# Soft-capped attention before two feed-forward layers: conversions by GpSimd, six key buffers, one transfer for sums, and the last pair's row sums on TensorE

## The chip, the cores and the metric

One Trainium2 chip, and one of its cores. The time is what the device takes for one launch, in microseconds (us). The kernel before takes 515.05 us, the median of 3 runs (514.95 to 515.98).

## The reference

Twelve heads in each of two batches, 448 positions, 64 channels a head. With `q` and `k` scaled so that the scores spread widely:

```python
scores = (q @ k.T) / sqrt(64)
scores = cap * tanh(scores / cap)              # cap is an input, 30.0
attn = exp(scores - max(scores))               # the kernel leaves the maximum out where cap bounds it
attn = attn / (sum(attn) + 1e-9)
x = (attn @ v), heads side by side             # 896 tokens x 768
x = relu(x @ w_in) ** 2 @ w_out                # 768 -> 2048 -> 768
x = silu(x @ w2_in) @ w2_out                   # 768 -> 2048 -> 768
```

All is float32 outside; the weights come as 64-bit floats and are turned into pairs of 16-bit floats (a high and a low part) on the chip.

## The kernel before

**Attention.** The 24 heads are 12 pairs; a pair shares a tile of 128 partitions, one head in the upper 64 channels and one in the lower. Two pairs make a round (`m`, 0 to 5), and a round has seven blocks of keys: A0, A1, A2 for the first pair, B0, B1, B2 for the second (128 keys each), and C, which holds the last 64 keys of both pairs, the first pair's in partitions 0 to 63 and the second pair's in 64 to 127. The 42 blocks are taken two at a time: a step `h` of the loop issues the scores of two blocks (TensorE, `scores`, L570), their tanh and exp (ScalarE, L584 and L679), and the products with the values of the two blocks of the step before (`values`, L586).

**Row sums.** VectorE adds the exponentials of a pair's blocks into `total` (`add`, L603), and TensorE multiplies `total` by a block of equal numbers (`ones`), which gives the sum over keys, repeated over rows. For the rounds 0 to 4 one bank of PSUM holds four sums (`add_up`, L615). VectorE copies it to `sm`, four transfers turn its four rows of 448 into a tile `st` of 32 partitions by 56 (L641), VectorE inverts that (L646, L647), it goes to DRAM (`scratch`, L648) and comes back repeated over 64 partitions (`rb`, L654), and the pair's output is multiplied by it (L659). For the last two pairs (10 and 11) the sums go through `add_up_pair` (L625) to a full bank each, `sump`, and VectorE inverts 128x448 numbers at once (`last_sums`, L662).

**What sets the order.** Each engine works its instructions in the order in which the program issues them, and so does the queue of SyncE, from which all the large transfers start. A tile takes the place of an older tile of its kind (`bufs` says how many there are), and waits for that tile's last reader. Keys and queries of a pair are one tile `qk`, with four places; `pr.load` (L513) is issued in the steps in which block C or B2 of a round is scored, for the two pairs of the next round.

**Weights.** `Stream` loads a weight tile (`raw`, three places, 768 KB each), takes its upper half as a 16-bit float into `top` (the tile `zeros`, one place; `head`, L306), lets VectorE shift the lower bits and join them (`shift`, L313, which writes `u`), and splits `u` into the high and low parts `hl`. Twelve such steps are issued one by one in the steps 5 to 16 of the attention (`ws.step`, L718), the first four conversions among them. After the attention a planner takes over: it keeps a clock for ScalarE and VectorE and, beside each piece of TensorE's work, issues the step that is open and due first (`chunk`, L467). The parts of the input `x0` that are still to be made are steps with due times too (`x0.late`).

**Feed-forward.** The first four output tiles are four sums of products (`plain`, L991): six units of twelve products first, of which four use only the pairs 0 to 7 and two need the pairs 8 to 11, then the next two tiles from whole inputs. TensorE's four banks for them are emptied by ScalarE before they are taken again.

Of the kernel before, what the change touches and what calls it, by code (L numbers as in the profile page):

```python
# [8 lines left out]
F32 = mybir.dt.float32  # L9
# [17 lines left out]
def softcap_attention_relu2_silu(  # L27
# [12 lines left out]
    nc = tc.nc  # L40
# [201 lines left out]
    class Stream:  # L242
# [53 lines left out]
        def turn_steps(self, i):  # L296
# [5 lines left out]
            def raw():  # L302
                self.load_to(i)
                return self.raw[i]

            def head():  # L306
                nc.scalar.activation(  # L307
                    top.bitcast(F16).rearrange("p (n w) -> p n w", w=2)[:, :, 1],
                    raw().bitcast(BF16).rearrange("p (n w) -> p n w", w=4)[:, :, 2],
                    AF.Copy,  # L310
                )

# [8 lines left out]

            a = Step("A", 1.4 * WT, head, [self.turned[i - BENT]] if i >= BENT else [])
            b = Step("D", WT, shift, [a], self.room)
# [182 lines left out]
    class Pairs:  # L506
# [6 lines left out]
        def load(self, i):  # L513
            t = self.pool.tile([128, 2, S], F32, tag="qk", bufs=4, name=f"qk{i}{self.tag}")
            nc.sync.dma_start(t[:, 0], q[i])
            nc.sync.dma_start(t[:, 1], k[i])
            self.qk[i] = t
# [18 lines left out]
    def attention_bounded(att, spool, ws, x0):  # L536
# [66 lines left out]
        def add(m, x):  # L603
            e, i = ex[m, x], None if x == "C" else pair_of(m, x)
            if x in ("A1", "B1"):
                t = total[i] = att.tile([128, 2, S], F32, tag=f"total{x[0]}", bufs=2, name=f"total{i}")
                nc.vector.tensor_tensor(t, ex[m, x[0] + "0"], e, op=ALU.add)  # L607
            if x == "A2" or x == "B2" and m < NQ - 1:
                nc.vector.tensor_tensor(total[i], total[i], e, op=ALU.add)  # L609
            if x in ("C", "B1"):  # L610
                b = int(x == "B1")
                t = total[2 * m + b][head(b)]
                nc.vector.tensor_tensor(t, t, ex[m, "C"][head(b)], op=ALU.add)  # L613
# [10 lines left out]

        def add_up_pair(i, parts):  # L625
            s = sums["p", i] = bank(f"sump{i}")
            for n, t in enumerate(parts):
                for j in range(2):
                    nc.tensor.matmul(
                        s[head(j), :S], lhsT=one, rhs=t[:, j], start=(n == 0), stop=(n == len(parts) - 1)  # L630
                    )

# [3 lines left out]
        def evacuate_sums(m):  # L636
            t = att.tile([128, S], F32, tag="sm", bufs=2, name=f"sm{m}")
            nc.vector.tensor_copy(t, sums.pop(m)[:, :S])
            st[m] = att.tile([32, S // 8], F32, tag="st", bufs=2, name=f"st{m}")
            for r in range(4):  # L640
                nc.sync.dma_start(  # L641
                    st[m][8 * r : 8 * r + 8], t[32 * r : 32 * r + 1].rearrange("o (a f) -> o a f", a=8)
                )

# [29 lines left out]
        for h in range(len(groups) + 1):  # L674
            if h < len(groups):
# [4 lines left out]
                for m, x in groups[h]:  # L680
                    if x in ("A0", "B0"):
                        i = pair_of(m, x)
                        if i + 2 < NP2:
                            pr.load_v(i + 2)
                    if x in ("C", "B2") and m + 1 < NQ:
                        pr.load(2 * m + 2 + (x == "B2"))
            if h == 1:
# [11 lines left out]
            for m, x in groups[h - 1] if h else []:  # L699
                values(m, x)  # L700
            for m, x in older:
                if x == "B2":
# [4 lines left out]
                    for b in range(2):  # L707
                        todo.append((lambda i=2 * m + b: normalise(i), h + 4 + 2 * b))
                if x == "C" and m == NQ - 1:
                    add_up_pair(last, [total[last]])  # L710
            if h in loads:
# [5 lines left out]
            if 5 <= h < 17:  # L717
                ws.step()  # L718
        add_up_pair(last + 1, [total[last + 1], ex[NQ - 1, "B2"]])
        for f, _ in todo:  # L720
            f()
        nc.scalar.activation(cell(last + 1), px.pop(last + 1)[:, :S], AF.Copy)
        x0.late(last_sums(last), last_sums(last + 1))

# [680 lines left out]
```

## Time and profile before

| what | value |
|---|---|
| median of 3 runs | 515.05 us |
| the profiled execution, its own time | 514.26 us |
| its span | 512.5 us |
| mean granted clock of TensorE | 0.992 of full speed |
| TensorE, matmuls | 501.1 us busy (98%), 2741 |
| VectorE | 353.0 us busy (69%), 668 |
| ScalarE | 337.2 us busy (66%), 516 |
| GpSimd | 24.1 us busy (5%), 28 |
| attention | from 5.4 us to about 90.6 us |
| feed-forward part | from about 90.6 us to the end |

The shares are means over stages with different limits, and a matmul counts as busy to its modelled end, so that 98% doesn't say that no time is lost. What is lost stands in the rows as a gap between the starts of TensorE's instructions, or in brackets behind an instruction: the time that its engine sat idle before it, and what ended that.

### The profile page before, as it was taken

To read this page: it belongs to the slowest core of one execution; us is meant where nothing else is said; L and a number is where in the kernel's file an instruction comes from. 1 tells how busy PE (TensorE), PEld (TensorE's weight loads), DVE (VectorE), ACT (ScalarE), POOL (GpSimd) and SP (SyncE) were. 2 spreads that over 40 slices of the span, in tenths; PEclk is the share of its full clock that TensorE was granted. 3 is DMA by queue.
4 is the path that set the end of the run, shared out by engine and by line. 5 is a ranking of instruction groups with operands and counts; after the bars stand their busy time and mean duration, and the time that the engine had idled before them with its cause. 6 is when DMAs were issued, how large, how long until landed. Compare 5 with 4: busy or idle time off the path is not lost.

```text
span 512.5 us, 7246 instructions
## 1 busy us (share of the span) xinstructions
PE 501.1 (98%) x2741; PEld 251.6 (49%) x2741; DVE 353.0 (69%) x668; ACT 337.2 (66%) x516; POOL 24.1 (5%) x28
## 2 busy tenths in 40 slices
PE   8999998999999999999999999999999999999995
PEld 4332232445555555555555555555666555556562
DVE  0769996898878677776779887889376278673110
ACT  5999898397778874448886757787555467860000
POOL 1003334300000000000000000000000000000000
PEclk9999999999999999999999999999999999999998
DMA  8546651233352355442453211336466013502111
GB/s 269 203 140 174 213 165 34 68 123 124 125 176 77 111 173 201 126 134 83 153 185 112 76 63 62 124 123 201 169 189 225 19 66 121 181 5 78 49 47 51
DMA packets 19357, 64.26 MB, mean 125 GB/s; under 512 B 2674, under 2 KB 11122, under 8 KB 19314
## 3 DMA queue, kind: packets, MB, share of 16 engines
q1 hardware_dynamic: 19280, 63.72, 37.8%
q8 instruction: 23, 0.38, 0.3%
q14 instruction: 20, 0.16, 0.1%
q0 software_dynamic: 32, 0.00, 0.0%
q10 hardware_dynamic: 2, 0.00, 0.0%
HBM read 60.88 MB, written 2.79 MB: 124 GB/s over the span
## 4 chain that ended last, share of the span: by engine, by line
PE 83%; DVE 10%; DMA 3%; SPq 2%; issue 1%; ACT 0%; DVEq 0%
PE yb_4f L858 4%; PE yb_5f L858 4%; PE yb_3f L858 4%; PE yb_0f L858 4%; PE yb_1f L858 4%; PE yb_2f L858 4%; PE yd_1f L1155 3%; PE yd_6f L1155 3%; PE yd_5f L1155 3%; PE yd_4f L1155 3%; PE yd_3f L1155 3%; PE yd_2f L1155 3%; PE yd_0f L1155 3%; SPq L641 2%; PE ha_1f L858 2%; DMA st<-sm 2%
## 5 line engine op out<-in xcount | busy, mean ns | idle before, releaser
L584 ACT ACTIVATE e_A<-s_A 128x896 f32<-128x896 f32 x18 | 16.0, 930 | 5.4 <-PE s_A L576 5.4
L584 ACT ACTIVATE e_B<-s_B 128x896 f32<-128x896 f32 x18 | 16.1, 936 | 1.4 <-PE s_B L576 1.2
L679 ACT ACTIVATE e_B<-e_B 128x896 f32<-128x896 f32 x18 | 16.7, 974 | 0.0
L679 ACT ACTIVATE e_A<-e_A 128x896 f32<-128x896 f32 x18 | 16.7, 970 | 0.0
L613 DVE TENSOR_TENSOR total<-total,e_C 64x896 f32<-64x896 f32 x12 | 13.4, 1114 | 0.4
L189 DVE SCALAR_TENSOR_TENSOR x1f<-yaf,x1f 128x448 f16<-128x448 f32 x15 | 9.2, 623 | 3.5 <-ACT x1f L799 3.4
L218 ACT ACTIVATE junk<-x0f 128x896 bf16<-128x896 f16 x6 | 5.7, 944 | 7.1 <-DVE x0f L804 6.8
L609 DVE TENSOR_TENSOR total<-total,e_A 128x896 f32<-128x896 f32 x6 | 8.2, 1360 | 0.3
L810 DVE TENSOR_TENSOR yaf<-yaf 128x448 f32<-128x448 f32 x12 | 7.2, 620 | 0.6 <-ACT yaf L799 0.6
L607 DVE TENSOR_TENSOR total<-e_A,e_A 128x896 f32<-128x896 f32 x6 | 6.6, 1103 | 1.2 <-ACT e_A L679 1.2
L799 ACT ACTIVATE x1f<-yaf 128x448 f16<-128x448 f32 x12 | 6.8, 570 | 0.8 <-DVE yaf L810 0.6
L646 DVE TENSOR_SCALAR st<-st,gcap 32x56 f32<-32x56 f32 x5 | 2.4, 471 | 7.0 <-DMA st<-sm 7.0
L1169 DVE SCALAR_TENSOR_TENSOR ycf<-yd_0f,ycf 128x384 f32<-128x384 f32 x2 | 1.1, 558 | 8.4 <-PE yd_0f L1155 8.4
L607 DVE TENSOR_TENSOR total<-e_B,e_B 128x896 f32<-128x896 f32 x6 | 6.7, 1122 | 0.0
L858 PEld LDWEIGHTS <-hl_0f 128*128 128x128 f16 x36 | 3.6, 102 | 5.4 <-issue 2.7
L667 DVE RECIPROCAL r<-r 128x448 f32<-128x448 f32 x2 | 5.9, 2954 | 0.1
L189 DVE SCALAR_TENSOR_TENSOR hl_63f<-u_63f,hl_63f 128x768 f16<-128x768 f32 x1 | 1.0, 958 | 7.2 <-ACT hl_63f L338 7.2
L679 ACT ACTIVATE e_C<-e_C 128x896 f32<-128x896 f32 x6 | 5.9, 977 | 0.0
L609 DVE TENSOR_TENSOR total<-total,e_B 128x896 f32<-128x896 f32 x5 | 5.5, 1091 | 0.4
L1169 DVE SCALAR_TENSOR_TENSOR ycf<-yd_4f,ycf 128x384 f32<-128x384 f32 x2 | 1.1, 558 | 6.7 <-PE yd_4f L1155 6.7
L1169 DVE SCALAR_TENSOR_TENSOR ycf<-yd_6f,ycf 128x384 f32<-128x384 f32 x2 | 1.1, 558 | 6.7 <-PE yd_6f L1155 6.7
L314 DVE SCALAR_TENSOR_TENSOR u_56f<-raw_wd_3f,zeros 128x768 int32<-128x768 int32 x1 | 1.0, 958 | 6.9 <-ACT zeros L307 6.9
(1820 smaller groups left out, 1659.2 us busy)
## 6 DMA issues: line engine op xcount, KB each, us to landing
out<-ycf SPq DMA_DIRECT2D x14, 192.0 KB
rb<-scratch SPq DMA_DIRECT2D x10, 224.0 KB
raw_wb_0f<-in_moe_w_out SPq DMA_DIRECT2D x2, 768.0 KB
raw_wb_1f<-in_moe_w_out SPq DMA_DIRECT2D x2, 768.0 KB
raw_wb_2f<-in_moe_w_out SPq DMA_DIRECT2D x2, 768.0 KB
raw_wb_3f<-in_moe_w_out SPq DMA_DIRECT2D x2, 768.0 KB
raw_wb_4f<-in_moe_w_out SPq DMA_DIRECT2D x2, 768.0 KB
raw_wb_5f<-in_moe_w_out SPq DMA_DIRECT2D x2, 768.0 KB
```

What stands on the lines that cost most here:

```text
L189: nc.vector.scalar_tensor_tensor(lo, x, scale, hi, op0=ALU.mult, op1=ALU.subtract, accum_out=watch.low() if see else None)
L584: nc.scalar.activation(t, sp[:, :, :S], AF.Tanh, scale=scale_s)
L607: nc.vector.tensor_tensor(t, ex[m, x[0] + "0"], e, op=ALU.add)
L609: nc.vector.tensor_tensor(total[i], total[i], e, op=ALU.add)
L613: nc.vector.tensor_tensor(t, t, ex[m, "C"][head(b)], op=ALU.add)
L641: nc.sync.dma_start(st[m][8 * r : 8 * r + 8], t[32 * r : 32 * r + 1].rearrange("o (a f) -> o a f", a=8))
L667: b = Step("D", 6 * S, lambda: nc.vector.reciprocal(t, t), [a])
L679: nc.scalar.activation(ex[m, x], ex[m, x], AF.Exp, scale=scale_c)
L799: return Step("A", cols, lambda: nc.scalar.activation(at(out), at(src), func, scale=scale), list(deps))
L810: return Step(eng, cols, lambda: e.tensor_tensor(at(out), at(x), at(y), op=op), list(deps))
L858: nc.tensor.matmul(acc, lhsT=w(e_w, kk), rhs=x(e_x, kk), start=first and i == 0, stop=last and i == len(n) - 1, skip_group_check=more,)
L1155: nc.tensor.matmul(acc[:, :NW], lhsT=g[KD * e + kk][:, e_g, t * 128 : t * 128 + 128], rhs=hl[:, e_w, kk * NW : kk * NW + NW], start=first ...
```

## The change

Four edits.

1. The first four conversions of weights (`head`) are GpSimd copies in place of ScalarE activations; in the planner's books they count as GpSimd's.
2. `qk` has six places in place of four, and the keys of the next round are asked for with blocks A1 and C in place of C and B2.
3. `evacuate_sums` moves the four sums with one transfer: four rows of the partitions 0, 32, 64 and 96, into 32 partitions.
4. The sums of the last two pairs: VectorE no longer adds the blocks of pair 11; TensorE multiplies each of its four blocks (C's lower half, B0, B1, B2) by `ones` and adds them up in PSUM. This and the product for pair 10 are issued one step earlier, among the values, and `last_sums(10)` stands ahead of the remaining multiplications in place of among the planner's steps.

```diff
--- before.py
+++ after.py
@@ -304,11 +304,12 @@
                 return self.raw[i]
 
             def head():
-                nc.scalar.activation(
-                    top.bitcast(F16).rearrange("p (n w) -> p n w", w=2)[:, :, 1],
-                    raw().bitcast(BF16).rearrange("p (n w) -> p n w", w=4)[:, :, 2],
-                    AF.Copy,
-                )
+                out = top.bitcast(F16).rearrange("p (n w) -> p n w", w=2)[:, :, 1]
+                src = raw().bitcast(BF16).rearrange("p (n w) -> p n w", w=4)[:, :, 2]
+                if i < 4:
+                    nc.gpsimd.tensor_copy(out, src)
+                else:
+                    nc.scalar.activation(out, src, AF.Copy)
 
             def shift():
                 nc.vector.scalar_tensor_tensor(
@@ -319,7 +320,7 @@
                 if self.loading:
                     self.load_to(i + self.nraw)
 
-            a = Step("A", 1.4 * WT, head, [self.turned[i - BENT]] if i >= BENT else [])
+            a = Step("A" if i > 3 else "P", 1.4 * WT, head, [self.turned[i - BENT]] if i >= BENT else [])
             b = Step("D", WT, shift, [a], self.room)
             self.turned.append(b)
             s, use = (i - 1, "s"), self.todo.use
@@ -511,7 +512,7 @@
             self.pool, self.tag, self.qk, self.vt, self.vc = pool, tag, {}, {}, {}
 
         def load(self, i):
-            t = self.pool.tile([128, 2, S], F32, tag="qk", bufs=4, name=f"qk{i}{self.tag}")
+            t = self.pool.tile([128, 2, S], F32, tag="qk", bufs=6, name=f"qk{i}{self.tag}")
             nc.sync.dma_start(t[:, 0], q[i])
             nc.sync.dma_start(t[:, 1], k[i])
             self.qk[i] = t
@@ -602,10 +603,12 @@
 
         def add(m, x):
             e, i = ex[m, x], None if x == "C" else pair_of(m, x)
+            if i == NP2 - 1:
+                return
             if x in ("A1", "B1"):
                 t = total[i] = att.tile([128, 2, S], F32, tag=f"total{x[0]}", bufs=2, name=f"total{i}")
                 nc.vector.tensor_tensor(t, ex[m, x[0] + "0"], e, op=ALU.add)
-            if x == "A2" or x == "B2" and m < NQ - 1:
+            if x in ("A2", "B2"):
                 nc.vector.tensor_tensor(total[i], total[i], e, op=ALU.add)
             if x in ("C", "B1"):
                 b = int(x == "B1")
@@ -622,13 +625,14 @@
                         s[at : at + 32, :S], lhsT=one[:, :32], rhs=total[2 * m + b][:, j], start=True, stop=True
                     )
 
-        def add_up_pair(i, parts):
-            s = sums["p", i] = bank(f"sump{i}")
-            for n, t in enumerate(parts):
-                for j in range(2):
-                    nc.tensor.matmul(
-                        s[head(j), :S], lhsT=one, rhs=t[:, j], start=(n == 0), stop=(n == len(parts) - 1)
-                    )
+        def add_up_pair(i, t, start=True, stop=True, part=slice(0, 128)):
+
+            if start:
+                sums["p", i] = bank(f"sump{i}")
+            for j in range(2):
+                nc.tensor.matmul(
+                    sums["p", i][head(j), :S], lhsT=one[part], rhs=t[part, j], start=start, stop=stop
+                )
 
         def evacuate(i):
             nc.vector.tensor_copy(cell(i), px.pop(i)[:, :S])
@@ -637,10 +641,8 @@
             t = att.tile([128, S], F32, tag="sm", bufs=2, name=f"sm{m}")
             nc.vector.tensor_copy(t, sums.pop(m)[:, :S])
             st[m] = att.tile([32, S // 8], F32, tag="st", bufs=2, name=f"st{m}")
-            for r in range(4):
-                nc.sync.dma_start(
-                    st[m][8 * r : 8 * r + 8], t[32 * r : 32 * r + 1].rearrange("o (a f) -> o a f", a=8)
-                )
+            rows = t.rearrange("(r o) (a f) -> r o a f", o=32, a=8)[:, 0]
+            nc.sync.dma_start(st[m], rows)
 
         def invert(m):
             nc.vector.tensor_scalar(st[m], st[m], gcap[:32], None, op0=ALU.add)
@@ -682,8 +684,8 @@
                         i = pair_of(m, x)
                         if i + 2 < NP2:
                             pr.load_v(i + 2)
-                    if x in ("C", "B2") and m + 1 < NQ:
-                        pr.load(2 * m + 2 + (x == "B2"))
+                    if x in ("A1", "C") and m + 1 < NQ:
+                        pr.load(2 * m + 2 + (x == "C"))
             if h == 1:
 
                 nc.vector.tensor_scalar(gcap, capt, -CAP_MAX, CAP_MAX, op0=ALU.max, op1=ALU.min)
@@ -698,6 +700,13 @@
                 add(m, x)
             for m, x in groups[h - 1] if h else []:
                 values(m, x)
+            for m, x in groups[h - 1] if h else []:
+                if m == NQ - 1 and x in ("C", "B0", "B1", "B2"):
+                    add_up_pair(
+                        last + 1, ex[m, x], x == "C", x == "B2", head(1) if x == "C" else slice(0, 128)
+                    )
+                if m == NQ - 1 and x == "C":
+                    add_up_pair(last, total[last])
             for m, x in older:
                 if x == "B2":
                     add_up(m)
@@ -706,8 +715,6 @@
                     todo.append((lambda m=m: fetch(m), h + 2))
                     for b in range(2):
                         todo.append((lambda i=2 * m + b: normalise(i), h + 4 + 2 * b))
-                if x == "C" and m == NQ - 1:
-                    add_up_pair(last, [total[last]])
             if h in loads:
                 ws.load_to(loads[h])
             for f, at in list(todo):
@@ -716,11 +723,12 @@
                     todo.remove((f, at))
             if 5 <= h < 17:
                 ws.step()
-        add_up_pair(last + 1, [total[last + 1], ex[NQ - 1, "B2"]])
+        for st_ in last_sums(last):
+            st_.fn()
         for f, _ in todo:
             f()
         nc.scalar.activation(cell(last + 1), px.pop(last + 1)[:, :S], AF.Copy)
-        x0.late(last_sums(last), last_sums(last + 1))
+        x0.late(last_sums(last + 1))
 
     def attention_general(att, spool, ws, x0):
         cell = x0.cell
```

TensorE at the end of the attention, before: `s5` are scores of the last round, `px` the outputs of the pairs 10 and 11, `sump` their row sums, `e5` the exponentials.

```order
L576 MATMUL s5_B2_763<-qk11f_686 128x448 x2
L595 MATMUL px10_715<-e5_C_726,vc5f_585 64x448 x2
L595 MATMUL px11_771<-e5_C_726,vc5f_585 64x448 x2
L595 MATMUL px11_771<-e5_B0_731,vt11f_653 64x448 x2
L595 MATMUL px11_771<-e5_B1_761,vt11f_653 64x448 x2
L595 MATMUL px11_771<-e5_B2_766,vt11f_653 64x448 x2
L629 MATMUL sump10_789<-total10_736,ones_149 64x448 x2
L629 MATMUL sump11_798<-total11_782,ones_149 64x448 x2
L629 MATMUL sump11_798<-e5_B2_766,ones_149 64x448 x2
```

And now:

```order
L577 MATMUL s5_B2_748<-qk11f_611 128x448 x2
L596 MATMUL px10_703<-e5_C_714,vc5f_576 64x448 x2
L596 MATMUL px11_756<-e5_C_714,vc5f_576 64x448 x2
L596 MATMUL px11_756<-e5_B0_719,vt11f_644 64x448 x2
L633 MATMUL sump11_763<-e5_C_714,ones_149 64x448 x2
L633 MATMUL sump10_766<-total10_724,ones_149 64x448 x2
L633 MATMUL sump11_763<-e5_B0_719,ones_149 64x448 x2
L596 MATMUL px11_756<-e5_B1_746,vt11f_644 64x448 x2
L596 MATMUL px11_756<-e5_B2_751,vt11f_644 64x448 x2
L633 MATMUL sump11_763<-e5_B1_746,ones_149 64x448 x2
L633 MATMUL sump11_763<-e5_B2_751,ones_149 64x448 x2
```

Five products for sums in place of three; three of them now stand between the values of B0 and of B1.

VectorE at the same place, before: `total11` is the sum of pair 11's blocks, `rb` the inverted sums of earlier rounds, `r` those of the last two pairs, `x0f` the 16-bit parts of the input.

```order
L607 TENSOR_TENSOR total11_782<-e5_B0_731,e5_B1_761 128x896
L613 TENSOR_TENSOR total11_782<-total11_782,e5_C_726 64x896
L659 TENSOR_TENSOR x8_c7f_125<-x8_c7f_125,rb3_697 128x448
L659 TENSOR_TENSOR x9_c8f_126<-x9_c8f_126,rb4_795 128x448
L659 TENSOR_TENSOR x10_c9f_127<-x10_c9f_127,rb4_795 128x448
L666 TENSOR_SCALAR r10_810<-sump10_789,gcap_148 128x448
L667 RECIPROCAL r10_810<-r10_810 128x448
L668 TENSOR_TENSOR x11_c10f_128<-x11_c10f_128,r10_810 128x448
L804 TENSOR_SCALAR x0f_117<-x11_c10f_128 128x448
L189 SCALAR_TENSOR_TENSOR x0f_117,lows_107<-x11_c10f_128,x0f_117 128x448
L666 TENSOR_SCALAR r11_811<-sump11_798,gcap_148 128x448
L667 RECIPROCAL r11_811<-r11_811 128x448
```

And now:

```order
L661 TENSOR_TENSOR x8_c7f_125<-x8_c7f_125,rb3_685 128x448
L668 TENSOR_SCALAR r10_789<-sump10_766,gcap_148 128x448
L669 RECIPROCAL r10_789<-r10_789 128x448
L670 TENSOR_TENSOR x11_c10f_128<-x11_c10f_128,r10_789 128x448
L661 TENSOR_TENSOR x9_c8f_126<-x9_c8f_126,rb4_786 128x448
L661 TENSOR_TENSOR x10_c9f_127<-x10_c9f_127,rb4_786 128x448
L812 TENSOR_SCALAR x0f_117<-x11_c10f_128 128x448
L189 SCALAR_TENSOR_TENSOR x0f_117,lows_107<-x11_c10f_128,x0f_117 128x448
L668 TENSOR_SCALAR r11_800<-sump11_763,gcap_148 128x448
L669 RECIPROCAL r11_800<-r11_800 128x448
L670 TENSOR_TENSOR x12_c11f_129<-x12_c11f_129,r11_800 128x448
L812 TENSOR_SCALAR x0f_117<-x12_c11f_129 128x448
```

The two additions for `total11` are gone, and the inversion for pair 10 stands ahead of the multiplications of the pairs 8 and 9, which wait for `rb4`.

The queue of SyncE around the keys of pair 8, before:

```order
L654 DMA rb1_471<-scratch_156 64x2x448 x2
L260 DMA raw_wb0_0f_493<-in_moe_w_out 128x6144
L515 DMA qk8f_513<-in_q 128x448
L516 DMA qk8f_513<-in_k 128x448
L522 DMA vt9f_516<-in_v 128x384
L641 DMA st2_533<-sm2_531 8x1x56 x4
L515 DMA qk9f_555<-in_q 128x448
L516 DMA qk9f_555<-in_k 128x448
```

And now:

```order
L656 DMA rb1_465<-scratch_156 64x2x448 x2
L516 DMA qk8f_481<-in_q 128x448
L517 DMA qk8f_481<-in_k 128x448
L260 DMA raw_wb0_0f_490<-in_moe_w_out 128x6144
L516 DMA qk9f_510<-in_q 128x448
L517 DMA qk9f_510<-in_k 128x448
L523 DMA vt9f_513<-in_v 128x384
L645 DMA st2_530<-sm2_528 32x1x56
```

The keys of the pairs 8 and 9 have moved ahead: pair 8's of the weight tile `raw_wb0_0`, pair 9's of the values of pair 9 and the transfer of sums, which is one transfer.

## Rows read from the trace of the kernel before

**Rows 1.** Who TensorE waited for over the whole span (us in total, times, longest)
```profile
PE sump L629 <- DVE total L613: 2.1, 1, 2.1
...
PE s_A L576 <- DMA qk8f<-in_k: 1.1, 1, 1.1
```

**Rows 2.** Stretch 80 to 90: engines busy, granted TensorE clock, DMA share, GB/s
```profile
80.00:90.00 10.00, 7.80 (x40) 2.17 (x36) 5.91 (x9) 8.30 (x13) 3.88 (x4) 0.91 0.19 49
```

**Rows 3.** Timeline 34 to 37 (start, us, engine, line, operation, [idle before])
```profile
34.41 1.15 ACT L307 ACTIVATE zeros<-raw_wa1f 128x768 f16<-128x768 bf16 x1
...
34.82 1.72 PE L595 MATMUL px<-e_A,vt4f 128*64 128x448 f32 x8
...
35.31 1.09 DVE L609 TENSOR_TENSOR total<-total,e_B 128x896 f32<-128x896 f32 x1
...
36.48 0.96 PE L621 MATMUL sum<-total,ones 128*32 128x448 f32 x8
```

**Rows 4.** Timeline, the keys of pair 8
```profile
48.99 0.43 SPq L516 DMA_DIRECT2D qk8f<-in_k  x1
...
57.00 1.77 PE L576 MATMUL s_A<-qk8f 64*128 64x448 f32 x8 [1.07 <-DMA qk8f<-in_k]
```

**Rows 5.** Timeline, the end of the attention on TensorE, ScalarE and VectorE
```profile
82.08 2.88 PE L595 MATMUL px<-e_B,vt11f 128*64 128x448 f32 x12
...
82.14 1.79 ACT L679 ACTIVATE e_B<-e_B 128x896 f32<-128x896 f32 x2
...
84.79 0.92 PE L629 MATMUL sump<-total,ones 128*64 128x448 f32 x4
...
86.58 1.09 DVE L613 TENSOR_TENSOR total<-total,e_C 64x896 f32<-64x896 f32 x1
...
87.81 1.35 PE L629 MATMUL sump<-total,ones 128*64 128x448 f32 x4 [2.10 <-DVE total L613]
...
88.89 1.76 PE L629 MATMUL sump<-e_B,ones 128*64 128x448 f32 x4
...
90.59 2.97 PE L858 MATMUL ha_0f<-x0f,hl_0f 128*128 128x448 f16 x12
```

**Rows 6.** Timeline, the way of the sums of a round of heads
```profile
30.98 0.24 DVE L646 TENSOR_SCALAR st<-st,gcap 32x56 f32<-32x56 f32 x1 [3.15 <-DMA st<-sm]
...
80.49 2.75 SPq L641 DMA_DIRECT2D st<-sm  x4
...
80.92 1.07 DVE L613 TENSOR_TENSOR total<-total,e_C 64x896 f32<-64x896 f32 x1
...
84.31 0.24 DVE L646 TENSOR_SCALAR st<-st,gcap 32x56 f32<-32x56 f32 x1 [2.32 <-DMA st<-sm]
...
91.48 0.63 DVE L659 TENSOR_TENSOR x_c8f<-x_c8f,rb 128x448 f32<-128x448 f32 x1 [3.15 <-DMA rb<-scratch]
```

**Rows 7.** Timeline, first products of the feed-forward part and the last reciprocal
```profile
98.61 2.95 DVE L667 RECIPROCAL r<-r 128x448 f32<-128x448 f32 x1
...
103.08 0.62 DVE L189 SCALAR_TENSOR_TENSOR x0f<-x_c11f,x0f 128x448 f16<-128x448 f32 x1
...
103.77 0.54 PE L858 MATMUL ha_1f<-x0f,hl_0f 128*128 128x448 f16 x2 [0.37 <-DVE x0f L189]
...
105.28 2.43 PE L858 MATMUL ha_0f<-x0f,hl_2f 128*128 128x448 f16 x12
```

**Rows 8.** Chain that ended last, one unit of twelve products
```profile
114.52 2.27 PE ha_0f L858 x12
```

**Rows 9.** GpSimd by line and shape (busy us, mean ns)
```profile
L1236 POOL TENSOR_SCALAR x0f<-x_c1f 128x448 f16<-128x448 f32 x1 | 0.6, 563 | 4.7 <-DVE x_c1f L659 4.7
...
L1237 POOL TENSOR_TENSOR x0f<-x_c3f,x0f 128x448 f16<-128x448 f32 x1 | 1.9, 1937 | 0.1
```

**Rows 10.** Timeline, GpSimd and VectorE side by side
```profile
49.93 1.75 POOL L1237 TENSOR_TENSOR x0f<-x_c1f,x0f 128x448 f16<-128x448 f32 x1
...
50.89 1.75 DVE L609 TENSOR_TENSOR total<-total,e_A 128x896 f32<-128x896 f32 x1
```

## The prediction

> **What bounds the kernel now.** I read the list of TensorE's waits first: over the whole span it names hardly more than 2.1 us for the sum of the last pair and 1.1 us for the keys of pair 8 [rows 1]. So TensorE sets the pace nearly everywhere, and a change pays only where one of its gaps closes or its own work changes. Then the table by stretches, for the clock: from 80 to 90 the granted clock is 0.91, TensorE is busy 7.8 of 10 us and the other engines are no fuller [rows 2]. The rest is the timeline around the places that the diff touches.
>
> In the middle of the attention TensorE isn't held up by the conversions on ScalarE: beside one of 1.15 us it goes from two blocks of values at 34.82 to the sum at 36.48 without a gap, 0.83 us a block [rows 3]. The end is different. The values of B0 start at 82.08 and the last block of values is followed by pair 10's sum at 84.79; then TensorE waits 2.10 us for VectorE's additions of pair 11, of which the last runs from 86.58 to 87.67; and the last sum, starting at 88.89, takes 1.76 us where the one at 84.79 took 0.92, so that it runs at the lower of the two clock levels (1.2 and 2.4 GHz) after that idle time. The first unit of the feed-forward part starts at 90.59 and still takes 2.97 us, against 2.43 for the same number of products at 105.28 [rows 5, 7].
>
> **The change part by part.**
>
> *Conversions to GpSimd.* Four ScalarE instructions of some 1.15 us go [rows 3]. I count nothing for that: TensorE, working without a gap beside them, is what hides them, and it stays. What they may cost lies on VectorE. A conversion of 768 elements on GpSimd isn't in the trace; its nearest rows are a one-input operation on 448 elements in 0.563 us, by elements 0.97 us for 768, and a two-input one beside a busy VectorE in 1.937 us, or 3.3 us [rows 9]. While a GpSimd subtraction ran from 49.93 to 51.68, VectorE's addition at 50.89 took 1.75 us in place of the 1.09 at 35.31 [rows 3, 10]: one of the two has to let the other pass. The Trainium skill, SBUF — State Buffer, section "Who interferes with whom", says that a VectorE instruction with two SBUF inputs and a GpSimd instruction that reads SBUF exclude each other for a whole instruction; the trace agrees (0.66 us lost), and the rule speaks against this edit.
>
> So I let each conversion cost VectorE between 0 and its whole length, and ask who waits for VectorE. The tightest place is the sum of the second round: its last addition ends at 35.31 + 1.09 = 36.40, and TensorE takes it at 36.48, 0.08 us later [rows 3]. But ahead of it VectorE sat idle for 3.15 us until 30.98, for the transfer of the first sums [rows 6], and 2.06 us of that go (next paragraph). So a conversion there may cost VectorE some 2.1 us before TensorE sees it. Of the ends 0.97 and 3.3 I take the first, for its row has one input as the conversion has: cost 0. The other end costs 3.3 - 2.1 = 1.2 us at this place, and at most as much again at each of two later conversions, 3.6 us in all. The first runs before VectorE has much to do.
>
> *One transfer for the sums.* The four take 2.75 us to issue from 80.49, 0.69 us each; VectorE has them at 84.31, 1.07 us after the last issue [rows 6]. One alone should be there 0.69 + 1.07 = 1.76 us after its start, 2.06 us sooner. What it moves is the same; that it is issued as fast with four times the pieces is an assumption, between 0 and 2.06 us of gain. This shortens VectorE's waits and brings `rb4` forward. By itself it is worth nothing to TensorE, but it pays for the conversions above.
>
> *Six places for keys.* Pair 8's keys are issued until 49.42 and TensorE stands until 57.00 for them, 1.07 us [rows 4]. Now they stand ahead of a weight tile of 768 KB, not behind it, and behind a fetch that starts 2 us sooner; SyncE's queue holds nothing in front of them that wasn't there before. The later keys are also asked for sooner. I take it that nothing else ends later there, since TensorE waited for nothing of the kind before or after. Gain: 1.1 us; at worst 0, if another wait stood close behind.
>
> *The end of the attention.* Before, from the values of B0 at 82.08 to the first unit at 90.59 it was 8.51 us; less B0's own 0.83, 7.68 [rows 5]. Now TensorE has seven blocks there: C's product for the sum, pair 10's sum, B0's product, values of B1 and B2, products of B1 and B2. Each has the form of a block of values, 0.83 us [rows 3], so 7 x 0.83 = 5.81. That is 1.66 us more work than before (two products), and 1.87 us less time. Are they fed? The exponentials of B1 and B2 end at 82.14 + 1.79 = 83.93 [rows 5], now 1.1 sooner, at 82.83; values of B1 come up at 82.91 - 1.1 + 3 x 0.83 = 84.30. Pair 10's sum comes up at 82.64 and needs VectorE's addition of C, which ended at 80.92 + 1.07 = 81.99 [rows 6] and now ends sooner, since VectorE follows TensorE. The first unit therefore starts at 82.91 - 1.1 + 5.81 = 87.6 in place of 90.59.
>
> With no gap left, the clock shouldn't fall: the wait of 1.07 us at 57.00 brought no slow products after it, whose eight take the usual 1.77 [rows 4]. So the first unit takes 2.43, not 2.97: gain 0.54.
>
> *Behind it.* Units that need pairs 8 to 11 come after four units of 2.27 us [rows 8], at 87.6 + 9.1 = 96.7; pair 11's are needed one unit later, 99.0. VectorE's path: `x_c8` waits for `rb4` and starts at 91.48 [rows 6], now 1.1 + 2.06 sooner, at 88.3; from its start to the low part of pair 11 there are eight short operations of about 0.63 and a reciprocal of 2.95 [rows 6, 7], 8.0 us, so 96.3. Pair 10's inversion is done by then, because its sum is ready at 83.5. So the wait of 0.37 at 103.77, for pair 11's low part, goes [rows 7]. What is late next is ScalarE: a high part (`hl_4`) is now ahead of the emptying of TensorE's banks, and needs VectorE to make `u_4`: three operations behind pair 11's low part, 0.63 + 2 x 0.95 (estimates by elements from 0.62 for 448), some 98.8, then 0.9 and 0.6 on ScalarE: 100.3. TensorE wants the first bank again at 87.6 + 6 x 2.27 = 101.2. It holds by 0.9 us.
>
> **Sum.** 1.1 (keys) + 1.87 (end) + 0.54 (clock) + 0.37 (pair 11) = 3.9 us. After that TensorE has no wait to speak of until the end [rows 1], so what it gains it keeps. The profiled execution took 514.26, so 510.4; the median is 0.8 above it, 515.05, and with the same 3.9 the forecast for a median is 511.2 us.
>
> **Rivals.**
>
> 1. *VectorE becomes the bound through the conversions.* For it: the addition of 1.75 us [rows 10] and the 0.08 us at 36.48 [rows 3]. Against it: the 2.06 us that the one transfer gives back. With conversions of 3.3 us and 1.2 lost at one to two places: 511.2 + 1.2 to 2.4 = 512.4 to 513.6.
>
> 2. *The new wait at the first bank.* If the one transfer of sums is no quicker than four, `x_c8` starts at 90.4, the first bank comes at 102.4 and TensorE waits 1.2 us; the clock may fall once more, for another 0.5: 512.4 to 512.9. For it: the order of ScalarE, and margins of 0.9 us only. Against it: the issue of 0.69 us for each.
>
> 3. *Slower.* The same lock as in 1, at a higher price: three conversions, each of d us, hold VectorE up by d - 2.1 each, and TensorE waits for sums and banks. All gain is gone when 3 x (d - 2.1) = 3.9, at d = 3.4, just beyond the longest row scaled (3.3). At 4.2 us each it would be 511.2 + 6.3 = 517.5. For it: both operands of the conversion are strided, as in no GpSimd row here. Against it: GpSimd would have to be over four times as slow per element as in 0.563 us for 448.
>
> 4. *Nothing to measure.* The gap at the end is closed, but the planner's other order of steps opens as many in the feed-forward part, where VectorE is full: 514 to 516. For it: the order of VectorE's steps is another one. Against it: TensorE waited there for nothing before, and VectorE reaches that part with two additions less to do.
>
> **How the numbers follow.** 0.2% of 515.05 is 1.03 us, about what can be told from no change: faster is below 514.0, slower above 516.1. The forecast within about 1.3 us gets 0.62 (509.9 to 512.5). Rivals 1 and 2 together 0.20, nearly all of it below 514.0. Nothing to measure 0.10, slower 0.08. Faster thus 0.82, same 0.10, slower 0.08. The range takes the forecast and rivals 1 and 2, from 509.8 (a little more gained from the clock and pair 11) to 514.2.
>
> **What would show it.** The list of TensorE's waits no longer has the keys of pair 8 nor an addition of pair 11; the stretch from 80 to 90 has a clock of 1.00; the first unit starts near 87.6 and the first product with `hl_2` near 101.4; conversions on GpSimd take about 1 us; VectorE's waits for `st` shrink by about 2 us each. The forecast is wrong if those conversions take 3 us or more and TensorE waits for `total` or a bank between 30 and 80, if the first unit starts after 89, or if new waits stand in the list after 101.

## The result, and the profile after

The changed kernel took 509.55 us (median of 4 runs, 509.31 to 509.89) against 515.51 for the kernel before in the same session (514.95 to 518.10); ratio 0.9875, 95% interval 0.984 to 0.991. The forecast was 511.2 with a range from 509.8. The direction was right; the time lies 0.25 us below the range. The experiments show that the edit to which the forecast gave nothing brings 4.9 us by itself, and that the other three together bring nothing without it. Where one execution of a kernel ran at a far lower granted clock (881.54 us at 0.56 with the end alone, 654.63 us at 0.75 with four transfers issued by GpSimd), it is left out of medians and ratios.

The profiled executions took 514.26 and 509.48 us, spans 512.5 and 507.4. Of TensorE's waits two are left after the change, which the kernel before has too; the sum and the keys of [rows 1] are gone (columns as there):

```profile
PE idle L91 <- DVE idle L88: 1.1, 1, 1.1
PE s_A L577 <- ACT e_A L585: 0.3, 1, 0.3
```

The stretch of [rows 2], after the change: TensorE is busy throughout, at a granted clock of 1.00 in place of 0.91 (columns: the stretch, its length, busy time of TensorE, its weight loads, VectorE, ScalarE and GpSimd, then as in [rows 2]).

```profile
80.00:90.00 10.00, 10.00 (x56) 3.71 (x50) 8.50 (x11) 6.68 (x12) 4.88 (x6) 1.00 0.43 126
```

TensorE's timeline after the change, for [rows 4, 5, 7]: the first scores with pair 8's keys, the seven blocks of the new end, the first unit, the first product with `hl_2`.

```profile
55.30 1.77 PE L577 MATMUL s_A<-qk8f 64*128 64x448 f32 x8
...
80.32 0.97 PE L596 MATMUL px<-e_B,vt11f 128*64 128x448 f32 x4
81.22 0.97 PE L633 MATMUL sump<-e_C,ones 64*64 64x448 f32 x4
82.12 0.97 PE L633 MATMUL sump<-total,ones 128*64 128x448 f32 x4
82.93 0.92 PE L633 MATMUL sump<-e_B,ones 128*64 128x448 f32 x4
83.68 1.67 PE L596 MATMUL px<-e_B,vt11f 128*64 128x448 f32 x8
85.18 1.67 PE L633 MATMUL sump<-e_B,ones 128*64 128x448 f32 x8
86.79 2.44 PE L866 MATMUL ha_0f<-x0f,hl_0f 128*128 128x448 f16 x12
...
100.42 1.87 PE L866 MATMUL ha_0f<-x0f,hl_2f 128*128 128x448 f16 x9
```

And the way of the sums, for [rows 6]: one issue of 0.58 us, and VectorE has them 80.24 - 78.49 = 1.75 us after its start (the forecast: 1.76; four took 84.31 - 80.49 = 3.82).

```profile
28.50 0.24 DVE L648 TENSOR_SCALAR st<-st,gcap 32x56 f32<-32x56 f32 x1 [0.90 <-DMA st<-sm]
...
78.49 0.58 SPq L645 DMA_DIRECT2D st<-sm  x1
...
80.24 0.24 DVE L648 TENSOR_SCALAR st<-st,gcap 32x56 f32<-32x56 f32 x1 [0.25 <-DMA st<-sm]
...
87.39 0.62 DVE L661 TENSOR_TENSOR x_c8f<-x_c8f,rb 128x448 f32<-128x448 f32 x1
```

Comparing the start of the same TensorE instruction in both traces gives a lead, which grows in few places: 0.23 us by the first values, 1.53 at arrivals of keys (1.14 of it at pair 8, the rest in gaps too small for the list of waits), 2.04 from the values of B0 to the first unit, 0.52 in that unit (2.97 to 2.44), 0.54 at pair 11. That is 4.86 us, unchanged from there to the last product; 0.24 more lies behind it. The 0.23 at the start isn't the edits': over all traces the first values start between 8.78 and 9.96.

### The profile page after: what moved, and what is told of

It is laid out like the page before. It is cut to its first block, busy times and chain, and to the rows that moved or that the text cites. A ratio compares the mean times of both kernels' runs of the same rounds, so it can differ in the third digit from the quotient of the medians.

```text
span 507.4 us, 7244 instructions
## 1 busy us (share of the span) xinstructions
PE 499.9 (99%) x2749; PEld 251.6 (50%) x2749; DVE 354.4 (70%) x671; ACT 332.6 (66%) x507; POOL 30.5 (6%) x32
## 4 chain that ended last, share of the span: by engine, by line
PE 98%; ACT 0%; DVE 0%; issue 0%
PE px L596 7%; PE yb_5f L866 4%; PE yb_4f L866 4%; PE yb_2f L866 4%; PE yb_3f L866 4%; PE yb_1f L866 4%; PE yb_0f L866 4%; PE s_B L577 3%; PE yd_1f L1163 3%; PE yd_6f L1163 3%; PE yd_5f L1163 3%; PE yd_4f L1163 3%; PE yd_3f L1163 3%; PE yd_2f L1163 3%; PE yd_0f L1163 3%; PE s_A L577 3%
## 5 line engine op out<-in xcount | busy, mean ns | idle before, releaser
L585 ACT ACTIVATE e_C<-s_C 128x896 f32<-128x896 f32 x6 | 5.5, 925 | 0.0
L91 PE MATMUL idle<-idle 128*128 128x256 bf16 x20 | 4.4, 416 | 1.1 <-DVE idle L88 1.1
L1163 PEld LDWEIGHTS <-gc0f 128*128 128x128 f16 x42 | 4.1, 98 | 2.8
```

The source lines that it names most:

```text
L585: nc.scalar.activation(t, sp[:, :, :S], AF.Tanh, scale=scale_s)
L1163: nc.tensor.matmul(acc[:, :NW], lhsT=g[KD * e + kk][:, e_g, t * 128 : t * 128 + 128], rhs=hl[:, e_w, kk * NW : kk * NW + NW], start=first ...
```

## The experiments

Theory 1 at the outset: each edit closes a gap of its own, and only the keys were priced too low. Rival: ScalarE was a part of the path, so the conversions gained too. Four kernels carry one edit each. The ratios are estimated from the single runs and aren't the quotients of the medians beside them. In the code, `...` stands for what is left out.

| kernel | median us | ratio to before, 95% interval |
|---|---|---|
| keys alone | 516.50 | 1.0015 (0.9990 to 1.0039) |
| conversions alone | 514.47 | 0.9991 (0.9965 to 1.0017) |
| one transfer alone | 510.31 | 0.9895 (0.9867 to 0.9923) |
| end alone | 515.23 | 0.9997 (0.9973 to 1.0020) |

(The kernel before: 515.17 in 29 runs, 513.31 to 518.18.)

**Keys alone.**
```diff
-t = self.pool.tile([128, 2, S], F32, tag="qk", bufs=4, ...)
+t = self.pool.tile([128, 2, S], F32, tag="qk", bufs=6, ...)
...
-if x in ("C", "B2") and m + 1 < NQ: ...
+if x in ("A1", "C") and m + 1 < NQ: ...
```


> The kernel before with the keys alone changed (six places, asked for earlier). The trace after gains 1.53 us on TensorE at arrivals of keys (0.19 at qk6, 0.14 at qk7, 1.14 at qk8, 0.06 at qk11), where 1.1 was forecast. Theory 1 (the keys were under-priced, because their late arrival also costs small gaps that no wait shows): 1.5 us faster in the profile, and 1.5 to 2.5 in the median, since the kernel before would lose its spread with these waits. Theory 2 (the keys are worth the 1.1 forecast, the rest comes from ScalarE without the conversions): 1.1 us faster, 0.22%, and the small gaps at qk6 and qk7 still there. Everything from pair 10's values to the end should lie as before: 8.5 us from the values of B0 to the first unit.

No gain. TensorE is 1.45 us ahead at pair 8's first scores, and no wait for keys is left. But 1.06 us of that are gone by pair 9's scores, because the sums ahead of them take 2.01 us in place of 0.96, and the wait for the last sum is 3.5 us in place of 2.1. TensorE and VectorE of this kernel, behind pair 8's scores and at the end of the attention:

```profile
58.42 0.24 DVE L646 TENSOR_SCALAR st<-st,gcap 32x56 f32<-32x56 f32 x1 [1.25 <-DMA st<-sm]
...
62.43 2.01 PE L621 MATMUL sum<-total,ones 128*32 128x448 f32 x8
...
85.31 0.24 DVE L646 TENSOR_SCALAR st<-st,gcap 32x56 f32<-32x56 f32 x1 [2.32 <-DMA st<-sm]
...
87.58 1.09 DVE L613 TENSOR_TENSOR total<-total,e_C 64x896 f32<-64x896 f32 x1
...
88.81 1.76 PE L629 MATMUL sump<-total,ones 128*64 128x448 f32 x4 [3.55 <-DVE total L613]
```

Both times the addition that TensorE needs stands on VectorE behind the inversion, and that behind the transfer. What TensorE gained at the keys it loses at these sums.

**Conversions alone.**
```diff
-nc.scalar.activation(..., AF.Copy)
+if i < 4:
+    nc.gpsimd.tensor_copy(out, src)
+else:
+    nc.scalar.activation(out, src, AF.Copy)
```


> The kernel before with the first four conversions alone on GpSimd, the four transfers of sums kept. Theory 1: nothing for TensorE, within 0.3 us of before, because TensorE worked beside the conversions without a gap. Theory 2 (ScalarE was not as free as forecast): 0.5 to 1.5 us faster, to be seen as gaps that close where the conversions of 1.15 us stood. The first rival of the prediction (VectorE held up by the lock, with nothing given back by the transfer): 0.5 to 1.5 us slower, with a wait for a total near 36 or 68 in the list.

Nothing that can be told from no change, as forecast. The interval still leaves room for the 0.5 to 1.5 us of the rival theory; that falls with the changed kernel without these conversions, below. Its trace has one wait that the kernel before hasn't, 1.1 us in front of pair 6's first scores; with the end alone and with four transfers by GpSimd, TensorE waits there for that pair's keys.

**One transfer alone.**
```diff
-for r in range(4):
-    nc.sync.dma_start(st[m][8 * r : 8 * r + 8], ...)
+rows = t.rearrange("(r o) (a f) -> r o a f", o=32, a=8)[:, 0]
+nc.sync.dma_start(st[m], rows)
```


> The kernel before with the four transfers of sums replaced by one. As forecast: VectorE has the sums about 2 us sooner, TensorE gains nothing before the feed-forward part; there the normalised pair 8 comes 2 us sooner, which may take off the wait of 0.37 us for pair 11's low part at 103.77 or part of it, so 0 to 0.4 us faster. If the rival is right that the sums are what the feed-forward part waits for, 0.5 us or more.

Expected 0 to 0.4 us, measured 4.9 in the median. Both gaps close with nothing else changed. SyncE issues pair 8's last keys at 46.95 where it was 48.99 [rows 4]. Of these 2.04 us, 1.08 come from the store of the inverted sums ahead of them (42.22 in place of 43.30) and 0.93 from pair 7's queries, whose issue took 1.35 us before and takes 0.42 here; why it was so long isn't shown. TensorE then has no wait for pair 8, and at the end VectorE and TensorE stand so:

```profile
46.95 0.42 SPq L516 DMA_DIRECT2D qk8f<-in_k  x1
...
55.31 1.77 PE L576 MATMUL s_A<-qk8f 64*128 64x448 f32 x8
...
80.26 0.24 DVE L644 TENSOR_SCALAR st<-st,gcap 32x56 f32<-32x56 f32 x1 [0.25 <-DMA st<-sm]
...
82.54 1.09 DVE L613 TENSOR_TENSOR total<-total,e_C 64x896 f32<-64x896 f32 x1
...
83.05 1.70 PE L629 MATMUL sump<-total,ones 128*64 128x448 f32 x8
...
84.55 0.95 PE L629 MATMUL sump<-e_B,ones 128*64 128x448 f32 x4
85.43 2.44 PE L856 MATMUL ha_0f<-x0f,hl_0f 128*128 128x448 f16 x12
```

The addition of [rows 5], 86.58 before, starts at 82.54: 4.04 us sooner, of which 2.07 is the idle time in front of the inversion (2.32 to 0.25) and the rest the earlier start of the transfer (78.51 in place of 80.49). TensorE doesn't wait there and the clock holds. By its own lead: 1.53 at keys, 3.42 at the end, 0.52 clock, less 1.15 that it loses again at pair 11.

**End alone.** Edit 4 as a whole, of which:
```diff
+if i == NP2 - 1:
+    return
...
+add_up_pair(last + 1, ex[m, x], x == "C", x == "B2", ...)
```


> The kernel before with the end of the attention alone changed (pair 11's sums by TensorE from the blocks). Forecast by its own terms: 1.87 (end) + 0.54 (clock) = 2.41 us, and the 0.37 of pair 11 only if the four transfers leave it; the trace after shows 2.04 + 0.52 + 0.54 = 3.1. If it needs the single transfer (the prediction's second rival, the first bank): some 1.2 us less, 1.2 to 1.9. If it gives 3.1 alone, the transfer is worth nothing to it.

No gain. The end itself behaves as forecast: 84.72 to 91.19 from the values of B0 to the first unit, 6.47 us as in the changed kernel. It is given back at the first bank, which is the prediction's second rival (priced at 1.2 us):

```profile
94.79 0.62 DVE L662 TENSOR_TENSOR x_c8f<-x_c8f,rb 128x448 f32<-128x448 f32 x1 [1.87 <-DMA rb<-scratch]
...
106.47 1.56 ACT L808 ACTIVATE ha_0f<-ha_0f 128x448 f32<-128x448 f32 x3
...
107.05 1.29 PE L867 MATMUL ha_0f<-x0f,hl_2f 128*128 128x448 f16 x6 [1.92 <-ACT ha_0f L808]
```

VectorE gets to the pairs late because the fetched rows `rb` come from the same late sums. In this execution TensorE also waited 1.6 us for pair 6's keys and 0.4 for pair 7's, which it didn't before. By its starts against those of the kernel before it is 2.64 us late at the last scores, makes up 2.95 by the last product ahead of the bank, and loses 2.08 at the bank; so the bank takes back some 70% of what the end gained, and the lateness from before outweighs the rest.

So theory 1 falls. New theory: the transfer is the root. Four land 2 us later than one; VectorE stands in front of its inversion with the additions queued behind it; SyncE's key loads stand behind the store of the inverted sums. Rival: SyncE's 2.75 us of issue are the cause, not the landing. The next three kernels ran beside the kernel before at 514.76 (23 runs, 513.42 to 517.62); so did the one with the old end, below.

**The changed kernel with four transfers.**
```diff
-rows = ...
-nc.sync.dma_start(st[m], rows)
+for r in range(4):
+    nc.sync.dma_start(st[m][8 * r : 8 * r + 8], ...)
```


> The changed kernel with the four transfers of sums kept: conversions, keys and end of the attention are changed as before. New theory (the transfer is the root: four land some 2 us later, VectorE stands in front of its inversion with the additions queued behind it, and SyncE's later loads stand behind the transfer and behind the store of the inverted sums): little of the gain is left, 513.5 to 516 us, with a wait for a bank (ha_0f emptied by ScalarE) of about 1.9 us near 100, as the kernel with the changed end alone has it. The prediction's theory (each edit closes a gap of its own, the transfer none): within 0.5 us of the changed kernel, 509.1 to 510.1.

515.48 us, ratio 1.0011 (0.9989 to 1.0033): the three other edits together are worth nothing without the fourth. Its list of TensorE's waits has the bank again, and one for a sum:

```profile
PE ha_0f L868 <- ACT ha_0f L809: 1.9, 1, 1.9
PE sum L624 <- DVE total L612: 1.3, 1, 1.3
```

**Inversion one step of the loop later, four transfers.**
```diff
-todo.append((lambda m=m: invert(m), h + 1))
-todo.append((lambda m=m: fetch(m), h + 2))
+todo.append((lambda m=m: invert(m), h + 2))
+todo.append((lambda m=m: fetch(m), h + 3))
```


> The kernel before, four transfers, but VectorE inverts the sums one half step later in the program's order (and rb is fetched one later), so that the additions stand in front of the inversion. If VectorE's standing idle for the sums is what made the last sum late: its 7.0 us of waits for st shrink to under 2, the wait of 2.1 us for the last sum goes, and the clock stays; gain 2.1 + 0.5 = 2.6, less what the later fetch of rb4 costs at the banks near 100 (0 to 2.1): 0.5 to 2.6 us faster than before. If it is SyncE's queue alone (2.75 us of issue): the wait for the last sum stays, no gain, 515.

529.00 us, ratio 1.0293 (1.0270 to 1.0317): both expectations missed. VectorE no longer waits for `st`, but for what follows from it, up to 7.02 us for `rb`; and SyncE holds pair 8's keys behind the late store. SyncE, TensorE and VectorE of this kernel:

```profile
45.13 0.63 DVE L659 TENSOR_TENSOR x_c0f<-x_c0f,rb 128x448 f32<-128x448 f32 x1 [4.95 <-DMA rb<-scratch]
...
50.43 0.32 SPq L648 DMA_DIRECT2D scratch<-st  x1
...
53.76 0.43 SPq L516 DMA_DIRECT2D qk8f<-in_k  x1
...
59.81 3.36 PE L576 MATMUL s_A<-qk8f 64*128 64x448 f32 x8 [3.06 <-DMA qk8f<-in_k]
```

It doesn't part the theories as it was meant to, because the fetch moved too. It does show that this later way of the sums is paid for at keys (3.1 and 1.0 us), at the last sum (2.9) and at pair 11 (2.7).

**Four transfers issued by GpSimd.**
```diff
-    nc.sync.dma_start(st[m][8 * r : 8 * r + 8], ...)
+    nc.gpsimd.dma_start(st[m][8 * r : 8 * r + 8], ...)
```


> The kernel before with the four transfers issued by GpSimd in place of SyncE: SyncE's queue is free of their 2.75 us, but VectorE still waits for four transfers. If SyncE's queue alone is the cause: as good as the single transfer, 510 to 511 us. If VectorE's wait is: the wait of some 2 us for the last sum stays, and only the keys can come sooner, 0 to 1.5 us faster than before (513.7 to 515.2), or slower where GpSimd's issue takes longer than SyncE's.

515.62 us, ratio 1.0023 (1.0009 to 1.0037). SyncE's queue is free of the 2.75 us and nothing is gained, so its issue time by itself isn't the cause. The landing didn't stay as it was, though: VectorE waits 10.1 us for `st` in all, more than before (7.0), and in the second and third round its inversion starts 5.88 and 5.08 us after the issue, where it was 3.91 and 3.83. In its last round GpSimd issues four in 2.08 us and VectorE has them 87.00 - 83.70 = 3.30 us after the start:

```profile
83.70 2.08 POOL L641 DMA_DIRECT2D st<-sm  x4 [1.91 <-DVE sm L638]
...
87.00 0.55 DVE L646 TENSOR_SCALAR st<-st,gcap 32x56 f32<-32x56 f32 x1 [2.06 <-DMA st<-sm]
```

**Two transfers.** The kernel before with two transfers of two rows each. It and the kernels with the old keys, with all conversions on ScalarE and with fewer products of zeros ran beside the kernel before at 515.47 (16 runs, 513.22 to 518.86).
```diff
-for r in range(4): ...
-    nc.sync.dma_start(st[m][8 * r : 8 * r + 8], ...)
+for r in range(2):
+    nc.sync.dma_start(st[m][16 * r : 16 * r + 16], rows[2 * r : 2 * r + 2])
```


> The kernel before with two transfers of the sums in place of four, nothing else. If what counts is when the sums land (0.69 us of issue for each transfer ahead of the last): they land 1.4 us sooner than with four and 0.7 later than with one; VectorE's waits for st fall from 7.0 to between 2 and 4 us, the wait of 2.1 us for the last sum to under 1, and the time lies between 510.3 and 515, nearer the first: 510.5 to 512.5. If one transfer is quicker for another reason (its shape), two give nothing like it: 514 to 516.

512.42 us, ratio 0.9939 (0.9915 to 0.9962): between the two, as expected from the landing. Issue 1.15 us, VectorE at 80.88, 2.33 after the start of the issue; its waits for `st` are 2.3 us in all and TensorE's for the last sum is shorter:

```profile
78.55 1.15 SPq L642 DMA_DIRECT2D st<-sm  x2
...
80.88 0.76 DVE L645 TENSOR_SCALAR st<-st,gcap 32x56 f32<-32x56 f32 x1 [0.83 <-DMA st<-sm]
...
84.91 0.97 PE L629 MATMUL sump<-total,ones 128*64 128x448 f32 x4 [0.90 <-DVE total L613]
```

From the start of the issue to VectorE's inversion in the last round it is 1.75, 2.33 and 3.82 us for one, two and four transfers by SyncE (3.30 for four by GpSimd), and in the first round 1.86, 2.42 and 4.11; the times go with it: 510.3, 512.4, 515.2 (515.6). In the three rounds between, VectorE doesn't wait at all where one transfer is the only edit.

**The changed kernel with one edit undone.** Old end, edit 4 undone as a whole, of which:
```diff
-add_up_pair(last + 1, ex[m, x], x == "C", x == "B2", ...)
+add_up_pair(last + 1, [total[last + 1], ex[NQ - 1, "B2"]])
```


> The changed kernel with the old end of the attention: pair 11's sums through VectorE's additions. New theory: the single transfer alone has closed the gap at the end, as where it stood alone, so 509.5 to 510.5, at most 0.8 from the changed kernel. The prediction's theory: 1.87 + 0.54 + 0.37 = 2.8 us are lost, 512.3.

509.63 us, ratio 0.9917 (0.9899 to 0.9934). Old keys (`bufs=4`, asked for at `C` and `B2`):
```diff
-t = self.pool.tile([128, 2, S], F32, tag="qk", bufs=6, ...)
+t = self.pool.tile([128, 2, S], F32, tag="qk", bufs=4, ...)
...
-if x in ("A1", "C") and m + 1 < NQ: ...
+if x in ("C", "B2") and m + 1 < NQ: ...
```


> The changed kernel with the old keys (four places, asked for later). New theory (with the sums landing early the keys come in time in any order): within 0.5 us of the changed kernel, 509.3 to 510.1. The prediction's theory (keys 1.1 us, as measured by the lead 1.5): 510.6 to 511.1, with gaps before qk6, qk7 and qk8.

509.79 us, ratio 0.9895 (0.9871 to 0.9919). All conversions on ScalarE:
```diff
-if i < 4:
-    nc.gpsimd.tensor_copy(out, src)
-else: ...
+nc.scalar.activation(..., AF.Copy)
```


> The changed kernel with all conversions on ScalarE. The prediction's price (nothing) and the run with the conversions alone (0.7 us in the median, inside its interval): 509.3 to 510.0. If ScalarE was a part of the path near the start or the end: 510 to 511, with gaps beside the conversions of 1.15 us.

509.43 us, ratio 0.9892 (0.9869 to 0.9915). All three lie within 0.25 us of the changed kernel's 509.55: each of the three edits can be undone alone. At the end one trade can be read from the leads: with one transfer alone (old end) TensorE reaches the first unit with a lead of 5.16 and loses 1.15 at pair 11; with the new end it has 3.80 there, because of two products more, and loses nothing. By `hl_2` it is 4.53 and 4.86.

**Fewer products of zeros**, on the changed kernel:
```diff
-for _ in range(20):
+for _ in range(14):
```


> The changed kernel with 14 products of zeros ahead of the first scores in place of 20. The first scores start at 5.43 behind them; in other runs, whose products of zeros ran at the higher clock, they started at 4.6 to 4.9 and the lead left after the first 10 us was 0.4 to 1.0 us. If nothing else is late there: 0.3 to 0.8 us faster than the changed kernel, 508.7 to 509.3. If the clock of the first scores falls for it (2.21 us in place of 1.77 for eight, as in the kernel before): no gain, 509.3 to 509.9.

510.12 us, ratio 0.9907 (0.9887 to 0.9928), nothing gained. The first scores start 1.38 us sooner, at 4.05, and take the usual 1.77; but pair 1's keys aren't there, and the first values start at 9.54, 0.01 sooner than after the change:

```profile
4.05 1.77 PE L577 MATMUL s_A<-qk0f 64*128 64x448 f32 x8
...
8.63 0.56 PE L577 MATMUL s_C<-qk1f 64*64 64x448 f32 x1 [0.64 <-DMA qk1f<-in_k]
...
9.54 1.72 PE L596 MATMUL px<-e_A,vt0f 128*64 128x448 f32 x8
```

## Why the prediction was wrong

- *One transfer: "by itself it is worth nothing to TensorE".* This step failed. Its duration was right to 0.01 us (1.75), and so was the 2.06 us that VectorE gets back. What was missed is who stands behind. The wait of 2.32 us in [rows 6] ends at 84.31; VectorE's additions of pair 11 follow without a gap, and TensorE waits 2.10 us for the last of them [rows 5]. The prediction read that wait as an amount of VectorE's work to be taken away, not as VectorE's wait passed on. With the one transfer alone the wait is gone, and so is the one for pair 8's keys: 4.9 us in the median where the term was nothing.
- *Keys, 1.1 us, and end, 1.87 + 0.54.* Each was read rightly as a gap, and priced as if its edit were the one way to close it. Each edit does close its gap: keys alone brings 1.45 us at pair 8, end alone 6.47 us in place of 8.51. Neither keeps it: the first is lost at the sum ahead of pair 9's scores (1.06 us) and at the last sum (3.5 us), the second mostly at the first bank (1.9). Shown by the single edits, and by the changed kernel with four transfers, where all three together give nothing. So it was luck that the sum of 3.9 came near the 4.86 measured on TensorE: it counts the right gaps, under edits that don't bring them by themselves.
- *Pair 11 and the first bank.* The second rival's condition (a transfer that is no quicker) didn't arise in the changed kernel, but set up with four transfers it brought the wait that the rival names: 1.9 us where it said 1.2, without a further fall of the clock. The time was then 515.48, not 512.4 to 512.9, because the other gains go too. With the one transfer the margin held: ScalarE empties the banks from 99.07, `hl_2` starts at 100.42 without a wait. (One slip in that sum: the two VectorE operations of 0.95 us aren't an estimate by elements from 0.62 for 448, which gives 1.06.)
- *Conversions, 0.* Right. They took 1.06 to 1.93 us and cost VectorE 0.3 to 0.6 us at three places of the changed kernel (additions of 1.35, 1.55 and 1.71 us that take 1.07 or 1.08 with one transfer alone). Neither adding nor undoing the edit moves the time, and no wait for a total between 30 and 80, the sign of the first rival, stands in the lists of the changed kernel or of the conversions alone.
- *Size.* On TensorE 4.86 us in place of 3.9: keys 0.43 more (small gaps at pairs 6, 7 and 11 that the list of waits doesn't show), end 0.17, pair 11 0.17, start 0.23 (not an edit's), clock 0.02 less. The last 0.24 us of the span lie behind TensorE's last product.
- *From profile to median.* Adding 0.8 us to the forecast for the median assumed that the kernel after would lie above its profile as the one before did. It doesn't: 509.55 against 509.48. Without it the range would have reached down to 509.0.

Three things stay open.

- *The spread.* The kernel before varies by 4 to 6 us from run to run, those with four transfers by SyncE by 3 to 6, the one with two by 3.2, those with one by 0.3 to 2.4 (the changed kernel by 0.6 in four runs). Late keys don't look like all of it: with six places the traces have no wait for keys, and the spread is 6.1 us with the keys alone and 4.2 in the changed kernel with four transfers. Where the traces with four transfers part is the second round's sums: from the start of the issue to VectorE's inversion it is 3.91 us before, 5.11, 5.09 and 5.80 with the keys, the conversions and the end alone, and 7.48 in the changed kernel with four transfers (lines below), while the other rounds have 3.8 to 4.1 in all five. With one trace of each this is a lead, not a shown cause.
- *How the landing costs time.* That 1.5 us come by way of the keys and 3.4 by way of VectorE's additions is read from one trace; no run changes one way without the other.
- *The last 0.7 us* between one transfer alone (510.31) and the changed kernel (509.55). The intervals don't tell them apart. The leads by `hl_2` give the new end 0.33 of it against one transfer alone, and 0.72 against the changed kernel with the old end; but the stretch behind TensorE's last product, 5.5 to 6.5 us over all traces, varies by more.

```profile
38.51 4.15 SPq L645 DMA_DIRECT2D st<-sm  x4
...
45.99 0.41 DVE L650 TENSOR_SCALAR st<-st,gcap 32x56 f32<-32x56 f32 x1 [1.40 <-DMA st<-sm]
```

## What to carry to other kernels

When TensorE waits for an engine, look at what that engine waited for just before, and follow it back until something was really busy: here two of TensorE's gaps, on different queues, had one small transfer behind both. Gaps with a common cause are not to be added up edit by edit, and an edit that closes only its own gap hands the time to the next wait. Undo each edit from the finished kernel too: any one of three could go here without a difference that can be told.

## What the runs showed of the hardware

A conversion of 768 elements on GpSimd, strided on both sides, took 1.06 us where no addition of VectorE was running as it began, and 1.92 and 1.93 where one was; the addition behind the one of 1.92, which began during the conversion, took 1.71 where it takes 1.08 without one. GpSimd and VectorE of the changed kernel:

```profile
30.14 1.06 POOL L310 CAST zeros<-raw_wa1f 128x768 f16<-128x768 bf16 x1 [16.07 <-DVE u_0f L315]
...
64.42 1.39 DVE L612 TENSOR_TENSOR total<-total,e_A 128x896 f32<-128x896 f32 x1
64.81 1.92 POOL L310 CAST zeros<-raw_wa3f 128x768 f16<-128x768 bf16 x1
65.91 1.71 DVE L616 TENSOR_TENSOR total<-total,e_C 64x896 f32<-64x896 f32 x1
```

Read in order, the conversion lets the addition end (65.81) and then takes 0.92, and the next addition lets the conversion end (66.73). That agrees, to some 0.2 us, with the rule of the Trainium skill that the prediction quotes (SBUF — State Buffer, "Who interferes with whom"): with the conversion's rest of 0.82 and 1.08 of its own the addition would take 1.90. What it costs here stays on VectorE.

The issue of a transfer between the same tiles went by instructions here and not by pieces, in the last round: 0.58 us for all four rows in one, 1.15 for two, 2.75 for four on SyncE, 2.08 for four on GpSimd.
